# Operands of three routing steps and the scheduler's durations in a fused attention and mixture-of-experts kernel

## The chip, the cores and the metric

The kernel runs on one core of a Trainium2 chip. The metric is device time in microseconds for one execution of the whole program. Engines are named as in the profile: PE (TensorE), DVE (VectorE), ACT (ScalarE), POOL (GpSimd), SP (SyncE, here an issuer of DMAs).

## What is computed

The reference, cut to the parts that bear on the change. Attention and a gated layer produce 2304 tokens of 512 values; then tokens are routed to eight experts, each with room for 288 of them, in the order of their logits.

```python
q_pool = q.reshape(4, 8, 576, 2, 64).mean(axis=3)
attn = softmax(scale * q_pool @ k^T); x = attn @ v      # 2304 tokens x 512
x = ((x @ w1) * (x @ w2) @ w3) @ w_out
logits = x @ w_gate                                      # 2304 x 8
cap = 2304 // 8
for idx in np.argsort(-logits.flatten()):
    tok, e = idx // 8, idx % 8
    if assigned[tok] >= 0 or counts[e] >= cap:
        continue
    assigned[tok] = e; counts[e] += 1
for e in range(8):
    h = np.maximum(x[assigned == e] @ moe2_w1[e], 0.0)
    out[assigned == e] = h @ moe2_w2[e]
```

## The kernel before

Every fp32 product is made of three matmuls on operands split into a high and a low part (names that end in h and l, or hi and lo): hi by hi, lo by hi, hi by lo. The split of a weight block `u` of an expert is `uh` (a rounding copy on ACT) and `ul` (the subtraction `u - uh`, on DVE for experts 0, 1, 6 and 7, on POOL for 2 to 5). SP loads the blocks, 512 KB each, 64 in all, into a few buffers in turn; a buffer is free again when its `ul` has been made.

Attention runs until about 500 us, the gated layer until about 765 us. Then three kinds of work run side by side until about 1064 us:

- the routing, mostly on DVE, with small matmuls on PE;
- the rest of the gated layer, `x2` (matmuls of 512 columns, the last ones of 256), on PE until about 933 us;
- from there the experts on PE: per expert 96 matmuls of 288 columns in layer 1 (`pb<-exh,uh` and the like), 96 in layer 2 (`pb<-ehh,uh`), and transposes of gathered tokens (`g`) and outputs (`ey`).

The routing has eight phases. Each of the phases 0 to 6 searches, for all experts at once, the logit from which on an expert is full. It takes eight rounds: DVE makes a mask (`rt_mask`), PE counts with it (the MASK matmuls `pt<-rt_oh,rt_mask`), DVE multiplies, reduces and compares (`rt_cnt`, `rt_own`), PE spreads the verdict (the OWN8 matmul `pt<-rt_own,rc_ones`), DVE narrows the threshold. The tail of a phase compares with the threshold (`rt_ge`, twice), sums (`rt_rows`), lets PE sum over the partitions (the ROWS matmuls `pt<-rt_rows,...`), runs a scan along each expert's tokens that a row of ones and zeros `rst` resets (`tensor_tensor_scan`), and updates the expert's room left (`rt_r`, `rem`), the logits `L`, the accepted tokens (`rt_acc`, and `A` on POOL) and `pend`, the experts that became full. `pick` then takes one full expert, and `lists` makes the list of its tokens: `sl_all`, `sl_rows`, a PE matmul on it, six `sl_oh`, PE's list matmuls (`pt<-sl_mv,sl_oh`), and from their result `sl_fl` and the index tile `idx`, with which POOL gathers the expert's tokens (`g<-x,idx`) and scatters its outputs. Phase 7 has no search: it adds the experts that never filled to `pend`, picks one and makes its list.

Small operands of the routing lie in SBUF tiles (`ring`) or in a PSUM bank (`at`, printed as `pt` in the profile). The order on each engine is fixed before the program is built: the class `Sched` takes all operations of this stage with an engine, a modelled duration and a priority, runs a list schedule in model time, and every engine then executes its instructions in that order. The modelled duration on DVE is 65 ns and 1.04 ns for each element of a partition; what is called a duration in this text's diff is that number of elements (`dve(144, ...)`). Instructions recorded in this way all have the line L113 in the profile.

Of the kernel before, what the change touches and what calls it, by code (L numbers as in the profile page):

```python
# [11 lines left out]
F32 = mybir.dt.float32  # L12
F32R = mybir.dt.float32r
BF16 = mybir.dt.bfloat16
# [761 lines left out]
def routing_consts(nc, pool, spare):  # L776
# [10 lines left out]
    c = {}  # L787
# [12 lines left out]
    c["rst"] = rst = pool.tile([128, 8, 18], F32, name="rc_rst")  # L800
# [75 lines left out]
def routing(nc, sch, rp, slots, bank, c, L, keyL, A, rows_of, idx, prio, prio_l):  # L876
# [6 lines left out]
    def ring(name, n, shape, dt):  # L883
        return make_ring(sch, rp, "rt_" + name, n, shape, dt)
# [11 lines left out]
    r_M, r_M1 = at("M", 1, [128, 1], I32), ring("M1", 1, [128, 1], I32)  # L896
    (grid1, _), (wd, _) = at("grid1", 1, [128, NTHR], I32)(), at("wd", 1, [128, 8], F32)()
# [23 lines left out]
    dve(8, lambda: nc.vector.tensor_copy(wd, c["wd"]), [], ["rt_consts"])  # L921
    dve(144, lambda: nc.vector.tensor_scalar(L, L, -1e34, 1e34, op0=OP.max, op1=OP.min), [keyL], [keyL])

    def pick(n):

        (sc, ksc), (top, kt), (own, ko) = r_sc(), r_top(), r_own()
        dve(8, lambda: nc.vector.scalar_tensor_tensor(sc, pend, 0.5, wd, op0=OP.is_gt, op1=OP.mult), [keyP, "rt_consts"], [ksc], pr=P_PICK)
        dve(8, lambda: nc.vector.tensor_reduce(top, sc, axis=AX.X, op=OP.max), [ksc], [kt], pr=P_PICK)
        dve(8, lambda: nc.vector.tensor_scalar(own, sc, top, None, op0=OP.is_equal), [ksc, kt], [ko], pr=P_PICK)
        dve(8, lambda: nc.vector.tensor_tensor(pend, pend, own, op=OP.subtract), [keyP, ko], [keyP], pr=P_PICK)  # L930
        dve(4, lambda: nc.vector.scalar_tensor_tensor(
            rows_of[n], top[:, :].to_broadcast([128, 4]), -512.0, c["row"], op0=OP.mult, op1=OP.add), [kt], [("rows_of", n)], pr=P_PICK)
        return own, ko

    lists = slot_lists(nc, sch, rp, slots, bank, c, A, idx, prio, prio_l)
    for ph in range(8):
        if ph == 7:
            dve(8, lambda: nc.vector.scalar_tensor_tensor(pend, rem, 1e8, pend, op0=OP.is_lt, op1=OP.add), [keyR, keyP], [keyP])
            own = pick(7)
# [16 lines left out]
        if ph < 7:  # L956
# [4 lines left out]
            for rd, b in enumerate(BITS):  # L961
# [4 lines left out]
                else:  # L966
                    thr, kth = r_thr()
                    if rd == 1:
                        link(T, lambda thr=thr, T=T, rd=rd, base=base: nc.vector.tensor_scalar(
# [11 lines left out]
                if 0 < rd < len(BITS) - 1:  # L981
                    G, kG = r_G()
                    dve(T, lambda G=G, rd=rd, base=base: nc.vector.tensor_scalar(
                        G, c["grid"][rd + 1][0], base, None, op0=OP.bitwise_xor), [kb], [kG])
                    sch.ops[-1].sdeps.add(cut)
# [48 lines left out]
            for x, op in ((0, OP.is_ge), (1, OP.is_equal)):  # L1034
                dve(144, lambda ge=ge, th=th, mu=mu, oh=oh, x=x, op=op: nc.vector.scalar_tensor_tensor(
# [9 lines left out]
            def f(ps=ps, rows=rows):  # L1045
# [7 lines left out]
                inc.rearrange("p e c -> p (e c)"), c["rst"].rearrange("p e c -> p (e c)"),  # L1053
                ge[:, 1].rearrange("p e c -> p (e c)"), 0.0, op0=OP.mult, op1=OP.add), [(kge, 1)], [kin])
# [24 lines left out]
            dve(144, lambda ac2=ac2, s=s: nc.vector.tensor_reduce(  # L1079
# [31 lines left out]
def slot_lists(nc, sch, rp, slots, bank, c, A, idx, prio, prio_l):  # L1111
# [11 lines left out]
    r_mv, r_fl = ring("mv", 2, [128, 2, 3, NC], BF16), ring("fl", 2, [96, 2, 3], F32)  # L1123

    def lists(n, own):
# [7 lines left out]
        dve(144, lambda: nc.vector.tensor_tensor(  # L1133
# [12 lines left out]
        dve(18, lambda: nc.vector.scalar_tensor_tensor(slot, inc, pre, s, op0=OP.add, op1=OP.mult), [ki, kp, ks], [ksl])  # L1146
# [16 lines left out]
        def f2():  # L1163
# [3 lines left out]
        dve(6, lambda: nc.vector.tensor_copy(fl.rearrange("p x g -> p (x g)"), ps2.tile[:96, 0:6]), [], [kf], uses=[ps2])  # L1167
        dve(3, lambda: nc.vector.scalar_tensor_tensor(idx[n], fl[:, 0], 256.0, fl[:, 1], op0=OP.mult, op1=OP.add),
            [kf], [("idx", n)])
# [673 lines left out]
```

## Time and profile before

| what | us |
|---|---|
| median of 3 runs | 1208.83 |
| the runs | 1206.01 to 1209.98 |
| profiled execution, its own time | 1207.23 |
| its span, first to last instruction | 1205.4 |

The profile shows one execution. The busy shares of section 1 of its page are means over the whole span; the stage that the change touches is a fourth of it and is read by windows and timelines. Rows of a timeline show the start of a group of like instructions, its length, engine and operation, output and inputs, their count, and in brackets how long the engine had been idle before and which instruction released it. Durations of matmuls are longer than their distance, since they are pipelined.

### The profile page before, as it was taken

The numbers are of one execution on the slowest core, as the hardware profiler recorded it, in microseconds if no ns is written. First come the engines' busy times: TensorE is split into PE (matmuls) and PEld (weight loads), VectorE is DVE, ScalarE is ACT, GpSimd is POOL, SyncE is SP. The second block draws the span as 40 slices with busy tenths as digits, with TensorE's granted clock in tenths as the row PEclk, the third lists the DMA queues.
The fourth block names the chain that finished last, engine by engine and source line by source line (L and its number), as shares of the span: only waits on it lengthen the run. The fifth ranks groups of instructions, "written<-read, shape, count | busy, mean of one in ns | idle before, by whom it ended". The sixth has DMA issues, their size and how long they took to land.

```text
span 1205.4 us, 24241 instructions
## 1 busy us (share of the span) xinstructions
PE 1155.2 (96%) x8377; PEld 1091.5 (91%) x8377; DVE 946.3 (79%) x2953; ACT 701.8 (58%) x1453; POOL 513.0 (43%) x561
## 2 busy tenths in 40 slices
PE   7999999999999999999999999999999798899996
PEld 5999999999999999899999999776778798899996
DVE  7999999999999999998777765588778988833541
ACT  6888888888888888754433344223222454445520
POOL 4566666666666665500000000224443357776110
PEclk9999999999999999999999999999999899999998
DMA  8676666666666743125556532553112465546520
GB/s 214 153 179 150 154 154 154 154 154 149 158 140 153 161 114 86 42 88 201 188 180 192 187 95 85 165 174 106 40 40 51 152 201 167 175 134 215 176 69 21
DMA packets 114219, 167.92 MB, mean 139 GB/s; under 512 B 47479, under 2 KB 77310, under 8 KB 114094
## 3 DMA queue, kind: packets, MB, share of 16 engines
q1 hardware_dynamic: 110926, 156.92, 48.1%
q0 software_dynamic: 3168, 9.44, 2.5%
q8 instruction: 66, 1.08, 0.4%
q14 instruction: 59, 0.48, 0.1%
HBM read 104.87 MB, written 22.48 MB: 106 GB/s over the span
## 4 chain that ended last, share of the span: by engine, by line
PE 79%; DVE 16%; DMA 2%; issue 1%; SPq 1%; POOL 0%; ACT 0%; DVEq 0%; POOLq 0%; ACTq 0%
PE pb L113 37%; PE s L590 12%; PE pt L614 7%; PE pt L664 6%; PE pt L113 6%; PE s L664 6%; DVE pt L113 4%; PE s L614 3%; DVE sl_oh L113 1%; DVE ul L113 1%; DVE p L600 1%; DVE rt_mask L113 1%; PE pt L543 1%; DVE cv_v L113 1%; DMA u<-in_moe_w_dram 1%
## 5 line engine op out<-in xcount | busy, mean ns | idle before, releaser
L600 DVE TENSOR_SCALAR_CACHE_REDUCE p<-s 128x384 f32<-128x384 f32 x432 | 229.9, 551 | 32.6 <-PE pt L614 12.4
L590 PE MATMUL s<-kst,qst 128*128 128x384 f32 x768 | 199.7, 359 | 4.9 <-DVE p L600 3.4
L605 ACT ACTIVATE p<-p,mn 128x1152 f32<-128x1152 f32 x144 | 181.2, 1258 | 24.0 <-DVE mn L603 22.0
L113 POOL TENSOR_TENSOR x2l<-hraw,x2h 128x512 fp32r<-128x512 f32 x36 | 46.5, 1294 | 301.0 <-PE pt L113 250.7
L113 PE MATMUL pb<-xhi,wh 128*128 128x288 f32 x512 | 155.8, 304 | 1.2 <-ACT wh L113 1.2
L113 PE MATMUL pb<-xhi,wl 128*128 128x288 f32 x512 | 150.9, 295 | 1.4 <-POOL wl L113 1.2
L113 PE MATMUL pb<-xlo,wh 128*128 128x288 f32 x512 | 150.7, 294 | 0.0
L590 PEld LDWEIGHTS s<-kst,qst 128*128 128x128 f32 x768 | 123.4, 190 | 11.0 <-DVE p L600 8.0
L614 PE MATMUL pt<-ident,p 128*128 128x128 f32 x879 | 132.0, 272 | 0.3 <-ACT p L605 0.3
L648 DVE TENSOR_TENSOR p_lo<-pt,p_hi 128x384 fp32r<-128x384 f32 x230 | 124.6, 551 | 0.7 <-ACT p_hi L331 0.7
L331 ACT ACTIVATE p_hi<-pt 128x384 fp32r<-128x384 f32 x230 | 106.7, 493 | 11.2 <-PE pt L614 10.9
L614 PEld LDWEIGHTS pt<-ident,p 128*128 128x128 f32 x879 | 106.7, 140 | 4.5 <-ACT p L605 0.5
L113 PEld LDWEIGHTS pb<-xhi,wh 128*128 128x128 f32 x512 | 96.3, 188 | 2.6 <-ACT wh L113 1.6
L113 PEld LDWEIGHTS pb<-xhi,wl 128*128 128x128 f32 x512 | 96.1, 188 | 1.8 <-POOL wl L113 1.4
L341 POOL TENSOR_TENSOR p_lo<-praw,p_hi 128x384 fp32r<-128x384 f32 x96 | 97.0, 1018 | 0.4
L113 PEld LDWEIGHTS pb<-xlo,wh 128*128 128x128 f32 x512 | 96.4, 188 | 0.0
L113 DVE SCALAR_TENSOR_TENSOR cv_v<-cv_raw,cv_v 128x512 int32<-128x512 int32 (+1 forms) x120 | 83.8, 706 | 5.6 <-ACT cv_raw L113 4.4
L113 ACT ACTIVATE uh<-u 128x1024 fp32r<-128x1024 f32 (+1 forms) x84 | 68.6, 852 | 24.4 <-DMA u<-in_moe_w_dram 21.0
L335 POOL CAST p_hi<-praw 128x384 fp32r<-128x384 f32 x96 | 47.6, 506 | 81.6 <-ACT praw L331 81.5
L113 POOL TENSOR_TENSOR ul<-u,uh 128x1024 fp32r<-128x1024 f32 (+1 forms) x41 | 77.2, 1912 | 9.7 <-ACT uh L113 9.5
L113 PE MATMUL pb<-exh,uh 128*128 128x288 f32 x248 | 78.9, 318 | 0.0
L113 PE MATMUL pb<-ehh,uh 128*128 128x288 f32 x256 | 78.6, 307 | 0.0
(315 smaller groups left out, 3189.5 us busy)
## 6 DMA issues: line engine op xcount, KB each, us to landing
u<-in_moe_w_dram SPq DMA_DIRECT2D x64, 512.0 KB, 3.5
cv_raw<-in_moe_w_dram SPq DMA_DIRECT2D x32, 512.0 KB, 3.9
vr<-in_v_dram SPq DMA_DIRECT2D x32, 288.0 KB, 5.1
kr<-in_k_dram SPq DMA_DIRECT2D x32, 288.0 KB, 5.9
kst<-kH SPq DMA_DIRECT2D x31, 288.0 KB, 4.1
kst<-kL SPq DMA_DIRECT2D x31, 288.0 KB, 5.2
qr<-in_q_dram SPq DMA_DIRECT2D x15, 576.0 KB, 6.2
w3t<-wg SPq DMA_DIRECT2D x16, 512.0 KB, 3.5
```

Source lines behind the costliest of these rows:

```text
L113: return f(*[x.get() if isinstance(x, Lazy) else x for x in a], **{n: x.get() if isinstance(x, Lazy) else x for n, x in k.items()})
L331: nc.scalar.activation(out, in_, AF.Copy)
L335: nc.gpsimd.tensor_copy(out, in_)
L341: (nc.vector if eng == "DVE" else nc.gpsimd).tensor_tensor(out, a, b, op=OP.subtract)
L543: nc.tensor.transpose(ps.tile[:, a * 128:(a + 1) * 128], r[:, 3 * c + a, :, :].rearrange("p h d -> p (h d)"), ident)
L590: nc.tensor.matmul(ps.tile[:, :384], a[:, :], b[:, cs], start=(n == 0), stop=(n == len(passes) - 1))
L600: sch.op("DVE", c_dve(384), lambda ps=ps, c=c, cs=cs: nc.vector.tensor_scalar(t[:, cs], ps.tile[:, :384], 1.0, BIG, op0=OP.mult, op1=OP.mi ...
L605: sch.op("ACT", c_act(S, psum=False, acc=True), lambda: nc.scalar.activation(t, t, AF.Exp, bias=mn[:, 3:4], scale=-1.0, accum_out=sm[0][:, ...
L614: nc.tensor.transpose(ps.tile[:, a * 128:(a + 1) * 128], t[:, b * 128:(b + 1) * 128], ident)
L648: sch.op("DVE", c_dve(384), lambda view=view, src=src: nc.vector.tensor_tensor(view(lo), src(), view(hi).bitcast(F32), op=OP.subtract), us ...
L664: nc.tensor.matmul(ps.tile[:, :n], vt[:, t, :, :], src[half][:, t, off:off + n], start=(half == 0 and t == 0), stop=(half == 1 and t == NT ...
```

## The change

It has two parts. In the first, three steps of the routing read one operand from PSUM that came from SBUF. The reset row `rst` is made in bf16, copied once into the PSUM bank, and the scan reads it there. In phase 7 the step that adds the unfilled experts to `pend` becomes two: a comparison of `rem` that writes into PSUM, and an addition. In `lists`, only half of the list matmuls' result is copied to SBUF (`sl_fl`), and the index step reads the other half from PSUM.

In the second part, seven numbers that the scheduler takes for durations are raised; the instructions themselves stay. These numbers change the order of all engines from 765 us on.

```diff
-    c["rst"] = rst = pool.tile([128, 8, 18], F32, name="rc_rst")
+    c["rst"] = rst = pool.tile([128, 8, 18], BF16, name="rc_rst")
...
+    rst = at("rst", 1, [128, 4 * NC], F32)()[0].bitcast(BF16)
...
+    dve(72, lambda: nc.vector.tensor_copy(rst.bitcast(I32), c["rst"].rearrange("p e c -> p (e c)").bitcast(I32)), [], ["rt_rst"])
     dve(144, lambda: nc.vector.tensor_scalar(L, L, -1e34, 1e34, op0=OP.max, op1=OP.min), [keyL], [keyL])
...
-        dve(8, lambda: nc.vector.tensor_scalar(own, sc, top, None, op0=OP.is_equal), [ksc, kt], [ko], pr=P_PICK)
+        dve(80, lambda: nc.vector.tensor_scalar(own, sc, top, None, op0=OP.is_equal), [ksc, kt], [ko], pr=P_PICK)
...
-            dve(8, lambda: nc.vector.scalar_tensor_tensor(pend, rem, 1e8, pend, op0=OP.is_lt, op1=OP.add), [keyR, keyP], [keyP])
+            open_, kop = r_pen()
+            dve(8, lambda open_=open_: nc.vector.tensor_scalar(open_, rem, 1e8, None, op0=OP.is_lt), [keyR], [kop])
+            dve(8, lambda open_=open_: nc.vector.tensor_tensor(pend, open_, pend, op=OP.add), [kop, keyP], [keyP])
...
-                        link(T, lambda thr=thr, T=T, rd=rd, base=base: nc.vector.tensor_scalar(
+                        link(T + 72, lambda thr=thr, T=T, rd=rd, base=base: nc.vector.tensor_scalar(
...
-                    dve(T, lambda G=G, rd=rd, base=base: nc.vector.tensor_scalar(
+                    dve(T + 72, lambda G=G, rd=rd, base=base: nc.vector.tensor_scalar(
...
-                dve(144, lambda ge=ge, th=th, mu=mu, oh=oh, x=x, op=op: nc.vector.scalar_tensor_tensor(
+                dve(300, lambda ge=ge, th=th, mu=mu, oh=oh, x=x, op=op: nc.vector.scalar_tensor_tensor(
...
-                inc.rearrange("p e c -> p (e c)"), c["rst"].rearrange("p e c -> p (e c)"),
-                ge[:, 1].rearrange("p e c -> p (e c)"), 0.0, op0=OP.mult, op1=OP.add), [(kge, 1)], [kin])
+                inc.rearrange("p e c -> p (e c)"), rst,
+                ge[:, 1].rearrange("p e c -> p (e c)"), 0.0, op0=OP.mult, op1=OP.add), [(kge, 1), "rt_rst"], [kin])
...
-            dve(144, lambda ac2=ac2, s=s: nc.vector.tensor_reduce(
+            dve(255, lambda ac2=ac2, s=s: nc.vector.tensor_reduce(
...
-        dve(144, lambda: nc.vector.tensor_tensor(
+        dve(240, lambda: nc.vector.tensor_tensor(
             al, A.rearrange("p e c -> p c e"), own[:, None, :].to_broadcast([128, NC, 8]), op=OP.mult), ["A", kown], [ka], pr=P_PICK)
...
-        dve(18, lambda: nc.vector.scalar_tensor_tensor(slot, inc, pre, s, op0=OP.add, op1=OP.mult), [ki, kp, ks], [ksl])
+        dve(90, lambda: nc.vector.scalar_tensor_tensor(slot, inc, pre, s, op0=OP.add, op1=OP.mult), [ki, kp, ks], [ksl])
...
-        dve(6, lambda: nc.vector.tensor_copy(fl.rearrange("p x g -> p (x g)"), ps2.tile[:96, 0:6]), [], [kf], uses=[ps2])
-        dve(3, lambda: nc.vector.scalar_tensor_tensor(idx[n], fl[:, 0], 256.0, fl[:, 1], op0=OP.mult, op1=OP.add),
-            [kf], [("idx", n)])
+        dve(3, lambda: nc.vector.tensor_copy(fl, ps2.tile[:96, 3:6]), [], [kf], uses=[ps2])
+        dve(3, lambda: nc.vector.scalar_tensor_tensor(idx[n], ps2.tile[:96, 0:3], 256.0, fl, op0=OP.mult, op1=OP.add),
+            [kf], [("idx", n)], uses=[ps2])
```

The new orders, at three places. The first is DVE's queue at the end of the search of phase 4, where PE passes from `x2` to expert 0: before, from the last threshold step (a write of one word into `pt_68`) to `rt_r`.

```order
L113 SCALAR_TENSOR_TENSOR pt_68<-rt_n_9312,pt_68 128x1
L113 SCALAR_TENSOR_TENSOR rt_ge_9494<-pt_68,rt_oh_9239 128x18x8 x2
L113 TENSOR_REDUCE rt_rows_9501<-rt_ge_9494 128x16
L113 SCALAR_TENSOR_TENSOR pt_68<-rc_rst,rt_ge_9494 128x144
L113 TENSOR_TENSOR ul_11013<-u_9775,uh_10998 128x1024
L113 TENSOR_TENSOR exl_11018<-pt_67,exh_11011 128x288
L113 TENSOR_TENSOR exl_11018<-pt_65,exh_11011 128x288
L113 SCALAR_TENSOR_TENSOR rt_y_9511<-rt_ge_9494,pt_68 128x144
L113 TENSOR_TENSOR rt_r_9515<-pt_66,rt_rem_9180 128x8
```

And with the change, from the third `ul` to `rt_r`; two more `ul` stand in the same round ahead of these rows.

```order
L113 TENSOR_TENSOR ul_11050<-u_9851,uh_11009 128x1024
L113 SCALAR_TENSOR_TENSOR rt_ge_9498<-pt_68,rt_oh_9241 128x18x8 x2
L113 TENSOR_TENSOR ul_11077<-u_11007,uh_11055 128x1024
L113 TENSOR_REDUCE rt_rows_9505<-rt_ge_9498 128x16
L113 SCALAR_TENSOR_TENSOR pt_68<-pt_68,rt_ge_9498 128x144
L113 SCALAR_TENSOR_TENSOR rt_y_9517<-rt_ge_9498,pt_68 128x144
L113 TENSOR_TENSOR ul_11090<-u_11043,uh_11080 128x1024
L113 TENSOR_TENSOR exl_11005<-pt_66,exh_10995 128x288
L113 TENSOR_TENSOR ul_11097<-u_11066,uh_11092 128x1024
L113 TENSOR_TENSOR exl_11005<-pt_66,exh_10995 128x288
L113 TENSOR_TENSOR ul_11128<-u_11085,uh_11110 128x1024
L113 TENSOR_TENSOR rt_r_9521<-pt_66,rt_rem_9180 128x8
```

Seven `ul` now stand ahead of `rt_r`, counted from the last round's mask, and one stood there before. The row on `pt_68` with 128x144 before `rt_y` is the scan.

The second place is phase 7: DVE from `sl_all` of the list before (phase 6's) on, before,

```order
L113 TENSOR_TENSOR sl_all_9569<-A,pt_68 128x144
L113 SCALAR_TENSOR_TENSOR rt_pend_9190<-rt_rem_9180,rt_pend_9190 128x8
L113 TENSOR_TENSOR A<-A,pt_68 128x144
L113 SCALAR_TENSOR_TENSOR pt_68<-rt_pend_9190,pt_68 128x8
L113 TENSOR_REDUCE pt_68<-sl_all_9569 128x18
L113 TENSOR_REDUCE pt_68<-pt_68 128x1
L113 TENSOR_REDUCE sl_rows_9583<-pt_68 128x1
```

and with the change.

```order
L113 TENSOR_TENSOR sl_all_9573<-A,pt_68 128x144
L113 TENSOR_TENSOR rt_pend_9190<-pt_68,rt_pend_9190 128x8
L113 TENSOR_TENSOR A<-A,pt_68 128x144
L113 SCALAR_TENSOR_TENSOR pt_68<-rt_pend_9190,pt_68 128x8
L113 TENSOR_REDUCE pt_68<-sl_all_9573 128x18
L113 TENSOR_REDUCE pt_68<-pt_68 128x1
L113 SCALAR_TENSOR_TENSOR ehl_11247<-pb_6477,ehh_11195 128x288
L113 TENSOR_SCALAR pt_68<-pt_68 128x8
L113 SCALAR_TENSOR_TENSOR rows_12425<-pt_68,rc_row 128x4
L113 TENSOR_REDUCE sl_rows_9589<-pt_68 128x1
```

The step that writes `rt_pend` reads `pt_68` where it read `rt_rem`; two `ehl` (one of them a few rows ahead of this piece), a step of `pick` and `rows` moved ahead of `sl_rows`. PE's queue around the matmul on `sl_rows` of phase 6, before,

```order
L113 MATMUL pb_6536<-exh_11271,uh_0_9687 128x288
L113 MATMUL pb_6536<-exl_11358,uh_0_9687 128x288
L113 MATMUL pb_6536<-exh_11271,ul_0_9746 128x288
L113 LDWEIGHTS rc_tris
L113 MATMUL pt_66<-sl_rows_9583,rc_tris 128x1
L113 MATMUL pt_67<-ident,ey_11341 96x128
L113 MATMUL pt_67<-ident,ey_11356 96x128
L113 MATMUL pt_67<-ident,ey_11440 96x128
L113 MATMUL pt_67<-ident,ey_11480 96x128
```

and with the change.

```order
L113 MATMUL pb_6514<-exh_11210,uh_11145 128x288
L113 MATMUL pb_6514<-exl_11293,uh_11145 128x288
L113 MATMUL pb_6514<-exh_11210,ul_11282 128x288
L113 LDWEIGHTS rc_tris
L113 MATMUL pt_67<-sl_rows_9589,rc_tris 128x1
L113 MATMUL pb_6514<-exh_11210,uh_11181 128x288
L113 MATMUL pb_6514<-exl_11293,uh_11181 128x288
L113 MATMUL pb_6514<-exh_11210,ul_11322 128x288
L113 MATMUL pb_6514<-exh_11210,uh_0_9645 128x288
L113 MATMUL pb_6514<-exl_11293,uh_0_9645 128x288
```

Twelve transposes of `ey`, of which four stood right behind `sl_rows` in the piece before, now stand ahead of it with 39 matmuls of expert work since the ROWS matmuls (42 before). From there on, 15 and 42 such matmuls follow up to the list matmuls of phase 6 (before: 12 transposes, 6 and 24), and 24 matmuls and 9 transposes from these to those of phase 7 (before: 24).

The third place is POOL in phase 5, where it starts on expert 2's weights, before,

```order
L113 TENSOR_TENSOR ul_0_9798<-u_11459,uh_0_9785 128x512
L113 TENSOR_TENSOR ul_1_9817<-u_11459,uh_1_9794 128x512
L113 TENSOR_TENSOR ul_11013<-u_11485,uh_10998 128x1024
L113 TENSOR_TENSOR ul_11036<-u_11534,uh_11016 128x1024
L113 TENSOR_TENSOR ul_11094<-u_11607,uh_11022 128x1024
L113 TENSOR_TENSOR ul_11107<-u_11640,uh_11073 128x1024
L113 TENSOR_TENSOR ul_11114<-u_11674,uh_11098 128x1024
L113 TENSOR_TENSOR A<-A,rt_acc_9529 128x144
L113 TENSOR_TENSOR ul_11194<-u_11711,uh_11141 128x1024
```

and with the change.

```order
L113 TENSOR_TENSOR ul_1_9837<-u_11394,uh_1_9793 128x512
L113 TENSOR_TENSOR ul_10997<-u_11512,uh_10983 128x1024
L113 TENSOR_TENSOR ul_11026<-u_11535,uh_11003 128x1024
L113 TENSOR_TENSOR ul_11050<-u_11561,uh_11009 128x1024
L113 TENSOR_TENSOR ul_11077<-u_11615,uh_11055 128x1024
L113 TENSOR_TENSOR ul_11090<-u_11649,uh_11080 128x1024
L113 TENSOR_TENSOR ul_11097<-u_11680,uh_11092 128x1024
L113 TENSOR_TENSOR ul_11128<-u_11721,uh_11110 128x1024
L113 TENSOR_TENSOR A<-A,rt_acc_9533 128x144
L113 TENSOR_TENSOR ul_11282<-u_11755,uh_11145 128x1024
```

`A` stood behind two `ul` of 512 columns and five of 1024; now one of 512 and seven of 1024 stand ahead of it, and another one of 512 columns ahead of three scatters before these rows.

## Rows read from the trace of the kernel before

**Rows 1.** Page, section 1: busy us, share of span, instructions.
```profile
PE 1155.2 (96%) x8377; PEld 1091.5 (91%) x8377; DVE 946.3 (79%) x2953; ACT 701.8 (58%) x1453; POOL 513.0 (43%) x561
```

**Rows 2.** Waits of TensorE, 765 to 1064: us in total, times, longest.
```profile
PE pt L113 <- DVE exl L113: 5.4, 2, 2.9
PE pt L113 <- DVE rt_oh L113: 4.6, 5, 1.2
```

**Rows 3.** TensorE timeline: start, us, what, xcount [idle before, releaser].
```profile
998.15 0.20 PE L113 MATMUL pt<-rt_rows,rc_neg 128*128 128x8 bf16 x2 [2.94 <-DVE exl L113]
...
1047.86 0.16 PE L113 MATMUL pt<-sl_rows,rc_tris 128*128 128x1 bf16 x1 [3.58 <-DVE sl_rows L113]
...
1061.62 1.86 PE L113 MATMUL pt<-sl_mv,sl_oh 128*96 128x6 bf16 x15 [2.26 <-DVE sl_oh L113]
```

**Rows 4.** Windows: us, busy of PE, PEld, DVE, ACT, POOL; PEclk, DMA, GB/s.
```profile
933.00:948.00 15.00, 8.60 (x54) 7.72 (x53) 13.56 (x43) 6.35 (x9) 6.05 (x6) 0.77 0.43 134
997.00:1002.00 5.00, 3.85 (x22) 3.83 (x22) 4.73 (x17) 1.76 (x4) 0.91 (x2) 0.66 0.47 173
1049.00:1053.00 4.00, 4.00 (x20) 3.84 (x20) 3.73 (x15) 1.40 (x4) 2.84 (x7) 0.57 0.75 274
```

**Rows 5.** VectorE timeline, 985 to 1070.
```profile
993.69 4.06 DVE L113 TENSOR_TENSOR_SCAN pt<-rc_rst,rt_ge 128x144 f32<-128x144 f32 x1
...
1004.92 0.42 DVE L113 TENSOR_TENSOR sl_all<-A,pt 128x144 f32<-128x144 f32 x1
...
1037.98 0.46 DVE L113 TENSOR_TENSOR_SCAN pt<-rc_rst,rt_ge 128x144 f32<-128x144 f32 x1
...
1042.06 0.18 DVE L113 TENSOR_SCALAR pt<-rt_U 128x18 f32<-128x18 f32 x1
...
1044.44 2.18 DVE L113 SCALAR_TENSOR_TENSOR rt_pend<-rt_rem,rt_pend 128x8 f32<-128x8 f32 x1
...
1048.29 0.14 DVE L113 TENSOR_TENSOR rt_pend<-rt_pend,pt 128x8 f32<-128x8 f32 x1
...
1053.26 0.46 DVE L113 SCALAR_TENSOR_TENSOR ehl<-pb,ehh 128x288 fp32r<-128x288 f32 x1 [0.43 <-ACT ehh L113]
...
1056.44 4.75 DVE L113 SCALAR_TENSOR_TENSOR idx<-sl_fl 96x3 int32<-96x3 f32 x1
1061.12 1.90 DVE L113 TENSOR_TENSOR sl_oh<-pt,rc_i 128x288 bf16<-128x288 f32 x5
```

**Rows 6.** GpSimd timeline, 985 to 1070.
```profile
984.41 13.01 POOL L113 TENSOR_TENSOR ul<-u,uh 128x512 fp32r<-128x512 f32 x6
1000.45 0.49 POOL L113 TENSOR_TENSOR A<-A,rt_acc 128x144 f32<-128x144 f32 x1 [3.03 <-DVE rt_acc L113]
...
1041.88 4.71 POOL L113 TENSOR_TENSOR ul<-u,uh 128x1024 fp32r<-128x1024 f32 x2
...
1056.48 4.70 POOL L113 TENSOR_TENSOR ul<-u,uh 128x1024 fp32r<-128x1024 f32 x2
```

**Rows 7.** Chain that ended last, behind the routing: start, us, what.
```profile
1071.87 11.95 PE pb L113 x90
...
1096.73 0.74 PE pt L113 x9
```

**Rows 8.** Timelines of VectorE, ScalarE, GpSimd, TensorE: phases 2, 4, 5.
```profile
869.37 0.16 DVE L113 TENSOR_TENSOR rt_r<-pt,rt_rem 128x8 f32<-128x8 f32 x1
...
874.23 0.27 PE L113 MATMUL pt<-rt_oh,rt_mask 128*90 128x48 bf16 x3 [0.88 <-DVE rt_oh L113]
...
938.08 1.21 DVE L113 TENSOR_TENSOR ul<-u,uh 128x1024 fp32r<-128x1024 f32 x1
...
943.36 1.06 ACT L113 ACTIVATE uh<-u 128x1024 fp32r<-128x1024 f32 x1 [4.67 <-DMA u<-in_moe_w_dram]
...
979.19 0.68 DVE L113 TENSOR_TENSOR ul<-u,uh 128x512 fp32r<-128x512 f32 x1
...
983.16 7.25 POOL L113 TENSOR_TENSOR ul<-u,uh 128x512 fp32r<-128x512 f32 x4
```

More of the change, by code (lines that the diff above doesn't have):

```diff
@@ L1122, in slot_lists @@
     r_oh, r_og = ring("oh", 1, [128, NC, 96], BF16), ring("og", 1, [128, NC, 3], F32)
-    r_mv, r_fl = ring("mv", 2, [128, 2, 3, NC], BF16), ring("fl", 2, [96, 2, 3], F32)
+    r_mv, r_fl = ring("mv", 2, [128, 2, 3, NC], BF16), ring("fl", 2, [96, 3], F32)
     def lists(n, own):
```

## Prediction

> **What bounds the kernel now.** I read the profile page first: TensorE is busy for 96% of the span, VectorE for 79% [rows 1]. So a change pays only where TensorE stands still, or where it runs at the lower of its two clock levels. Next I asked which waits stop it in the stage that the change touches, from 765 us, where routing starts, to 1064 us, where the last list is made. The table of waits names VectorE in its longest rows [rows 2]. Then I looked at the three longest of these gaps: 2.94 us at 998, 3.58 us at 1048, 2.26 us at 1062 [rows 3]. After the first two the granted clock falls to its lower level: the mean is 0.66 over 997 to 1002 and 0.57 over 1049 to 1053 [rows 4], which costs 5 x 0.34 and 4 x 0.43, 1.7 us each. I take the same behind the third, where the clock falls too.
>
> What was VectorE doing? Each time one instruction took many times its usual length [rows 5]. The scan, 0.46 us in phase 6, took 4.06 us in phase 5; the step on `pend` took 2.18 us where another of its size takes 0.14; the index step, on 96 x 3 elements, took 4.75 us. (A row gives start and length: 993.69 + 4.06 = 997.75.) All three read both operands from SBUF. Beside each, GpSimd ran subtractions `ul`, and the long instruction ended when that row of subtractions ended [rows 6]: 997.75 against 997.42, 1046.62 against 1046.59, 1061.19 against 1061.18. In the same stretches instructions with one operand in PSUM keep their length, such as the 0.14 us one in [rows 5]. So the trace bears out that these three wait for GpSimd, and that reading one operand from PSUM frees them.
>
> **The change part by part.** All terms are against the profiled execution, 1207.2 us, which is 1.6 below the median and inside the runs' spread of 4 us. About 0.3% of the time, 3.6 us, is what a measurement can tell from no change.
>
> *The scan of phase 5.* It shrinks by 4.06 - 0.46 = 3.6 us. TensorE's gap behind it, 2.94 us, goes, and with it the 1.7 us of half clock: **-4.6**. Bounds: 0 (the wait stays) and -4.6. Next late there would be GpSimd's `A`, see the first rival.
>
> *The index step of phase 7.* It shrinks by 4.6 us; behind it stand the five `sl_oh` for which TensorE waited 2.26 us. What hides the new chain is 24 matmuls and 9 transposes between the two groups of list matmuls, about 3.9 us at the pace of [rows 7] (90 matmuls in 11.95 us, 0.133 each; 9 transposes in 0.74, 0.082 each), against six `sl_oh` of 0.38 us [rows 5] and the two steps on `sl_fl` and `idx`, some 2.7 us, on VectorE. The gap and the clock loss go: 2.26 + 1.7, **-4.0**; bounds 0 and -4.0.
>
> *The step on `pend`.* It is split in two: 2.18 becomes about twice 0.16, 1.9 less. But in the new order two `ehl` of 0.46 us each [rows 5] and two small steps, 0.2 each by their like, now stand ahead of `sl_rows`, for which TensorE waits. And TensorE does twelve transposes before that wait instead of behind it, worth 1.0 us, with three matmuls fewer, 0.4. (Only one of the `ehl` and both small steps come behind the `pend` step; the other `ehl` comes shortly before it, on the same chain.) The wait becomes 3.58 - 1.9 + 0.9 + 0.4 - 0.6 = 2.4 us. A gap of 2.26 us still halved the clock, so I give back only the idle time: **-1.2**, with bounds 0 and -5.3 (all of the gap and of the clock).
>
> *The tails of phases 0 to 3.* The raised durations put four more 512-column matmuls between a phase's last round and the next phase's first, where TensorE waits for `rt_oh`, 4.6 us in five waits [rows 2]. Two of the four stand ahead of the ROWS matmuls and so delay the chain that they cover; two stand behind. I take half of it for four phases: **-1.8**, bounds 0 and -3.6.
>
> *The turn from `x2` to the experts (phase 4).* Here the order moves most. Four phases with four more matmuls each empty `x2` one round earlier, and expert 0 starts a round earlier in routing's terms. VectorE gets seven `ul` ahead of `rt_r` where it had one [rows 8]. I worked this out from the mask of the last round, M. In the trace the first `ul` ends at 938.08 + 1.21 = 939.29 and gives its buffer to the fourth's weights; ScalarE's `uh` on these starts at 943.36, after waiting 4.67 us for the load. So one turn of the buffers takes 4.1 (load) + 1.06 (`uh`) + 1.22 (`ul`) = 6.4 us. In the new order the first `ul` ends at M + 1.8, the fourth can end at M + 8.2, and the seventh, whose buffer the fourth frees, at M + 14.8. `rt_r` comes then, where before it came right after the first. The next mask follows 4.9 us later, as in phase 2 (`rt_r` at 869.37, TensorE's mask matmul at 874.23), near M + 20. TensorE meanwhile has 48 matmuls of expert 0 ahead of ROWS and 51 behind (before: none and 48), so it reaches that mask near M + 16.5 and waits some 3.6 us, where it waited 2.4 (`exl`, the 5.4 less 2.9 in [rows 2]). From 933 to 948 TensorE was busy for 8.60 of 15 us at a clock of 0.77 [rows 4]; of the 6.4 us idle I take 0.6 off, since the ROWS matmuls now have work ahead of them and the other stops stay. So 1.2 - 0.6: **+0.6**. The bounds are wide: -4 if the clock stays up (15 x 0.23 = 3.4) and the stops shrink once more by 0.6, +6 if the clock is lost for as long again and the mask's wait doubles (3.4 + 2.4).
>
> *Additions.* One copy of 72 words in the head of routing, with the `rc_wd` copy now ahead of the first step on `L`, and dependences on them: by 0.14 to 0.18 us for a small step [rows 5] that is **+0.5** with a wait, bounds +0.2 and +1.0. The scan's reset row from PSUM I price at nothing, since the steps with a PSUM operand in [rows 5] are as short as those without; the index step's copy gets smaller. [...]
>
> Sum: -4.6 - 4.0 - 1.2 - 1.8 + 0.6 + 0.5 = -10.5, so 1207.2 - 10.5 = **1196.7 us**. A cross-check by TensorE's own work: behind the last group of list matmuls the new order leaves 54 matmuls of 0.133 us and 9 transposes less, 7.9 us; the groups would have to come 2.6 us sooner to give the same.
>
> **The rivals.**
>
> *GpSimd's `A` takes the scan's place.* In phase 5 `A` stood behind two half and five full `ul`, which ended at 997.42 [rows 6]; now one half and seven full, 2.4 us each, stand there in one row, so it may come some 4 us later, and `sl_all` behind it waits. VectorE had 4 us to spare at `A` (1000.45 to 1004.92), of which the shorter scan takes 3.6. For it: the row is longer. Against: expert 2's `ul` may start earlier. Price: up to 2 us of wait and the 1.7 of clock: **1200**.
>
> *More gain.* The transition loses its half clock and the `pend` gap falls under what halves it: -4.6 (0.6 to -4) and -4.1 (-1.2 to -5.3) on the sum: **1188**.
>
> *The operands don't free it.* If the new instructions wait as the old did, only the order counts: -1.8 + 0.6 + 0.5, and -0.6 for the transposes ahead of `sl_rows`: **1206**. The row nearest to the new `pend` step is `TENSOR_SCALAR` from `rt_U` into PSUM, 0.18 us at 1042.06, beside a GpSimd row of `ul` [rows 5, 6]; it did not wait. [...]
>
> *Slower: VectorE's own `ul` get caught.* They read `u` and `uh`, both from SBUF, and are untouched. Expert 1's last one ended at 979.19 + 0.68 [rows 8], 3.3 us before GpSimd's row for expert 2 began at 983.16. The experts now run 51 matmuls, 6.8 us, ahead of routing. If GpSimd's row starts before that last `ul`, VectorE is held until the row ends, as the scan was. Price: a row of seven `ul` of 2.4 us is 16.8, less the 0.7 of its own length, plus 1.7 of clock: 1196.7 + 17.8 = **1214**. It decides from an overlap on; with a row as in [rows 6], 13.01, it would end at 1210. Against it: in the new order GpSimd still does a single `ul` and three scatters before the row.
>
> **How the numbers follow.** My case 0.58, `A` 0.14, more gain 0.12, not freed 0.09, caught 0.07. My case's own range is 1191 to 1203, from the transition's +6 and the bounds of the `pend` and tail terms; the range 1187 to 1206.5 takes in the first three and most of the fourth. Faster than 1205.2: the first three less 0.05 for their upper ends, plus 0.02: 0.81. Within 0.3%: 0.05 + 0.06 = 0.11. Slower than 1212.5: the last case's 0.07 and 0.01 for a bad turn, 0.08.
>
> **What would show it.** All seven scans near 0.46 us and all eight index steps near 0.16; no `exl` or `sl_oh` gap over 1 us at phases 5 and 7; a gap for `sl_rows` of 2 to 3 us, still with half clock; `rt_r` of phase 4 some 14 us behind its mask, with a wait for `uh` before it. Wrong if a scan or index step is still several us long, if `sl_all` waits for `A`, or if a `ul` on VectorE takes more than 2 us.

## The result, and the profile after

| kernel | median us | runs | ratio to before, 95% interval |
|---|---|---|---|
| before | 1209.35 | 4 | |
| changed | 1197.2 | 4 (1190.61 to 1198.9) | 0.9898 [0.9861, 0.9934] |
| changed, again, beside 29 runs of before | 1199.37 | 12 (1196.52 to 1204.84) | 0.9930 [0.9907, 0.9953] |

The change makes the kernel 8 to 12 us faster by these ratios; a time of 1196.7 was forecast. The execution profiled first is the fastest of them, 1190.61 us with a span of 1188.7, so its rows show more gain than the medians. These are, of the changed kernel, section 1 of the page and then the waits of TensorE from 765 to 1064 us (in total, times, longest):

```profile
PE 1148.6 (97%) x8377; PEld 1085.6 (91%) x8377; DVE 934.5 (79%) x2955; ACT 702.7 (59%) x1453; POOL 518.3 (44%) x561
```

```profile
PE pt L113 <- DVE rt_own L113: 3.1, 7, 0.9
PE pt L113 <- DVE rt_oh L113: 3.0, 5, 0.7
...
PE pt L113 <- DVE exl L113: 1.7, 1, 1.7
PE pt L113 <- DVE sl_rows L113: 1.6, 1, 1.6
PE pt L113 <- DMA g<-x,idx: 1.2, 1, 1.2
```

Against [rows 2] the wait for `exl` fell from 5.4 to 1.7 us, that for `rt_oh` from 4.6 to 3.0. The wait for `sl_oh` is no longer there; the one for `sl_rows` was 3.58 [rows 3] and is 1.6. TensorE's timeline at what remains in phases 5 and 7:

```profile
984.20 0.21 PE L113 MATMUL pt<-rt_own,rc_ones 98*128 98x120 f16 x1 [0.92 <-DVE rt_own L113]
...
1043.47 0.18 PE L113 MATMUL pt<-sl_rows,rc_tris 128*128 128x1 bf16 x1 [1.62 <-DVE sl_rows L113]
```

Windows of the turn, behind the 984 gap, at `sl_rows` and at the last list (columns as in [rows 4]):

```profile
930.00:945.00 15.00, 9.82 (x59) 8.80 (x60) 13.53 (x37) 7.60 (x11) 6.92 (x6) 0.77 0.59 197
982.00:987.00 5.00, 4.08 (x33) 3.94 (x32) 3.46 (x15) 3.15 (x7) 4.27 (x2) 1.00 0.56 170
1043.00:1047.00 4.00, 3.53 (x27) 3.47 (x28) 3.86 (x20) 0.64 (x2) 3.98 (x4) 1.00 0.80 225
1057.00:1062.00 5.00, 5.00 (x42) 5.00 (x41) 0.77 (x3) 1.86 (x4) 4.86 (x5) 1.00 0.63 213
```

The clock, at 0.66 and 0.57 in [rows 4], is full at all three places behind the turn. VectorE's and GpSimd's timelines, for comparison with [rows 5, 6]:

```profile
994.78 0.45 DVE L113 TENSOR_TENSOR_SCAN pt<-pt,rt_ge 128x144 f32<-128x144 bf16 x1
...
1001.39 0.42 DVE L113 TENSOR_TENSOR sl_all<-A,pt 128x144 f32<-128x144 f32 x1
...
1038.38 0.17 DVE L113 TENSOR_SCALAR pt<-rt_rem 128x8 f32<-128x8 f32 x1
...
1041.44 0.16 DVE L113 TENSOR_TENSOR rt_pend<-pt,rt_pend 128x8 f32<-128x8 f32 x1
...
1052.73 0.15 DVE L113 SCALAR_TENSOR_TENSOR idx<-pt,sl_fl 96x3 int32<-96x3 f32 x1
...
1057.29 0.16 DVE L113 SCALAR_TENSOR_TENSOR idx<-pt,sl_fl 96x3 int32<-96x3 f32 x1
```

```profile
993.00 4.77 POOL L113 TENSOR_TENSOR ul<-u,uh 128x1024 fp32r<-128x1024 f32 x2 [0.21 <-ACT uh L113]
997.74 0.48 POOL L113 TENSOR_TENSOR A<-A,rt_acc 128x144 f32<-128x144 f32 x1
...
1037.24 2.40 POOL L113 TENSOR_TENSOR ul<-u,uh 128x1024 fp32r<-128x1024 f32 x1
...
1051.40 9.76 POOL L113 TENSOR_TENSOR ul<-u,uh 128x1024 fp32r<-128x1024 f32 x6 [0.79 <-ACT uh L113]
```

The scan of phase 5 (994.78) and the last two index steps (1052.73 for the list of phase 6, whose index step was the one held for 4.75 us in [rows 5], and 1057.29 for that of phase 7) run inside GpSimd's rows of `ul` (993.00 to 997.77, 1051.40 to 1061.16) and take 0.45, 0.15 and 0.16 us. The comparison of `rem` (1038.38), with its result in PSUM, takes 0.17 beside the `ul` from 1037.24. That is the plainest sign that the operand in PSUM frees them. The addition to `pend` (1041.44) met no `ul` in this order, so its 0.16 us says nothing. On VectorE the turn went as worked out:

```profile
933.25 0.44 DVE L113 TENSOR_TENSOR rt_mask<-pt,rt_thr 128x270 bf16<-128x270 f32 x1
933.80 1.22 DVE L113 TENSOR_TENSOR ul<-u,uh 128x1024 fp32r<-128x1024 f32 x1
...
947.67 1.22 DVE L113 TENSOR_TENSOR ul<-u,uh 128x1024 fp32r<-128x1024 f32 x1 [1.64 <-ACT uh L113]
948.81 0.16 DVE L113 TENSOR_TENSOR rt_r<-pt,rt_rem 128x8 f32<-128x8 f32 x1
```

`rt_r` comes 15.6 us behind the last round's mask (forecast 14.8), behind seven `ul`, the last of which waited 1.64 us for its `uh`.

All gaps of TensorE over 0.15 us from 760 us on sum to 27.1 us before and 15.0 after; the time at half clock (in 1 us windows from 700 to 1180 us the granted clock is 1.00 or 0.50, and between them where it changes), summed over these windows as the missing share, is 10.2 against 3.4 us. Together that is 19 us, where the spans differ by 16.7.

### The profile page after: what moved, and what is told of

It is laid out like the page before. It is cut to its first block, busy times and chain, and to the rows that moved or that the text cites. A ratio compares the mean times of both kernels' runs of the same rounds, so it can differ in the third digit from the quotient of the medians.

```text
span 1188.7 us, 24244 instructions
## 1 busy us (share of the span) xinstructions
PE 1148.6 (97%) x8377; PEld 1085.6 (91%) x8377; DVE 934.5 (79%) x2955; ACT 702.7 (59%) x1453; POOL 518.3 (44%) x561
## 4 chain that ended last, share of the span: by engine, by line
PE 80%; DVE 12%; DMA 3%; issue 2%; ACT 1%; POOL 1%; SPq 0%; DVEq 0%; POOLq 0%; ACTq 0%
PE pb L113 37%; PE s L590 13%; PE pt L614 7%; PE pt L664 6%; PE pt L113 6%; PE s L664 5%; PE s L614 3%; DVE pt L113 3%; DMA u<-in_moe_w_dram 1%; DVE sl_oh L113 1%; DVE p L600 1%; DVE rt_mask L113 1%; DVE ul L113 1%; PE pt L543 1%; DVE cv_v L113 1%
```

## The experiments

**Theory.** The three steps are held by GpSimd's subtractions as long as two operands are in SBUF; freeing them is worth 9.8 of the 10.5 us, and the order little. **Rival.** The order pays: it fills the tails, and takes the steps out of GpSimd's rows.

**1. The changed kernel again** (no edit).

> The changed kernel once more, to see how far its executions spread. Its profiled execution took 1190.6 us, the other runs 1196 to 1199. Theory: the same static order stands still for 14 to 15 us between 765 us and the end each time; where an execution is 6 to 8 us slower, TensorE's clock fell behind one or two more of the gaps (1.7 us each) and a gap near a DMA landing grew by some us. Rival: the executions differ before 765 us, in attention, and the change has no part in it; then the gaps from 765 us on would be the same and the start of routing (765 us) would be later. Median expected: 1196 to 1198.

The ratio is 0.9930 and the median 1199.37 us, 1.4 above what was expected. The profiled execution has a span of 1196.0, 7.3 more than the first. Until 500 us both keep TensorE busy alike (487.97 and 487.19 us), and routing starts at 765 us in both (`rt_pend` is set to zero at 765.24 and 765.71). From 760 us on the gaps are 19.2 against 15.0 us, and the half clock 6.8 against 3.4. So the theory held on where executions differ, not on how little: the largest difference is in phase 5. From the timelines of TensorE, VectorE, ScalarE and GpSimd of this execution:

```profile
986.26 0.21 PE L113 MATMUL pt<-rt_own,rc_ones 98*128 98x120 f16 x1 [2.75 <-DVE rt_own L113]
```

```profile
985.05 0.46 DVE L113 SCALAR_TENSOR_TENSOR ehl<-pb,ehh 128x288 fp32r<-128x288 f32 x1 [3.44 <-ACT ehh L113]
```

```profile
983.66 1.06 ACT L113 ACTIVATE uh<-u 128x1024 fp32r<-128x1024 f32 x1 [4.08 <-DMA u<-in_moe_w_dram]
```

```profile
975.05 2.21 POOL L113 DMA_INDIRECT out_dram<-eo,idx  x1 [0.23 <-issue]
...
978.51 3.65 POOL L113 TENSOR_TENSOR ul<-u,uh 128x512 fp32r<-128x512 f32 x2
```

And SyncE's loads (`q` marks an instruction that only issues a transfer):

```profile
979.83 2.69 SPq L113 DMA_DIRECT2D u<-in_moe_w_dram  x3
```

Read backwards: TensorE waits 2.75 us for `rt_own` (0.92 in the first execution); VectorE's `rt_own` stands behind an `ehl` that waits 3.44 us for ScalarE; ScalarE's `ehh` stands behind a `uh` that waits 4.08 us for its load. The next loads were issued from 979.83 on, 3.8 us before that `uh` began, when the first of the two `ul` from 978.51 had ended. These `ul` came late since three scatters stood ahead of them on GpSimd, one 2.21 us long. In the first execution the same scatters took 0.98, 0.92 and 1.62 us (here 1.50, 2.21 and 0.92), and the load was issued at 978.33. That this load is the one that the `uh` waited for is read from the order of the issues.

**2. The order with the old operands, pend step split.** The scan's and the index step's operands go back to SBUF (the reset row stays in bf16, here and in 8 and 10), and the comparison writes to SBUF:

```diff
+    rst_sb = c["rst"].rearrange("p e c -> p (e c)")
...
-            open_, kop = r_pen()
+            open_, kop = rp.tile([128, 8], F32, name="rt_open"), r_pen()[1]
...
-                inc.rearrange("p e c -> p (e c)"), rst,
+                inc.rearrange("p e c -> p (e c)"), rst_sb,
...
-        dve(3, lambda: nc.vector.scalar_tensor_tensor(idx[n], ps2.tile[:96, 0:3], 256.0, fl, op0=OP.mult, op1=OP.add),
+        dve(3, lambda: nc.vector.scalar_tensor_tensor(idx[n], fl[:, 0], 256.0, fl[:, 1], op0=OP.mult, op1=OP.add),
```

> The new order (all seven raised durations and the two extra instructions) with the three old operands: scan, index step and pend step read both operands from SBUF. Theory (the operands matter, the waits are for GpSimd's subtractions): the scan of phase 5 falls into a row of ul again and takes 2 to 4 us, an index step at the end of phase 6 or 7 takes 4 to 8 us, the pend step is free here because no ul runs beside it in the new order; time 1202 to 1209. Rival (the order is what paid, by 5 us or more from fuller tails and the turn at phase 4): scan and index step stay short because the new order takes them out of GpSimd's rows; time 1196 to 1199.

The ratio is 1.0013 [0.9988, 1.0037], the time 1209.89 us. From VectorE's timeline:

```profile
1024.34 4.31 DVE L113 SCALAR_TENSOR_TENSOR idx<-sl_fl 96x3 int32<-96x3 f32 x1
...
1053.95 2.25 DVE L113 TENSOR_SCALAR rt_open<-rt_rem 128x8 f32<-128x8 f32 x1
```

The theory seemed to hold, with one index step over 4 us, although the scan of phase 5 took 0.96 us where 2 to 4 were expected. But the second row is a step that neither kernel has: the comparison of `rem`, one operand, written to SBUF, was held too, where the theory had it free. So this run may not show the order alone (see 10).

**3. The operands with the old order.** All seven numbers go back, as in

```diff
-                dve(300, lambda ge=ge, th=th, mu=mu, oh=oh, x=x, op=op: nc.vector.scalar_tensor_tensor(
+                dve(144, lambda ge=ge, th=th, mu=mu, oh=oh, x=x, op=op: nc.vector.scalar_tensor_tensor(
```

> The three new operands with the old durations, so the order of before with two more small instructions. Theory (operands): no scan over 0.5 us, no index step over 0.2 us, the gaps for exl at phase 5 (2.94) and for sl_oh at phase 7 (2.26) gone, the gap for sl_rows at most 1.8 us, tails as before with 0.85 us for rt_oh each; 11 to 12 us less than before: 1197 to 1199. Rival (order): less than half of the gain, 1203 to 1207.

The ratio is 0.9918 [0.9895, 0.9942], the time 1197.59 us, as the theory has it. There is no scan over 0.456 us, no index step over 0.158, and at the end of routing one gap over 1 us is left:

```profile
1042.77 0.16 PE L113 MATMUL pt<-sl_rows,rc_tris 128*128 128x1 bf16 x1 [1.80 <-DVE sl_rows L113]
```

**4. The kernel before without `ul` on GpSimd.**

```diff
-        lo_e = ("POOL",) if FILLED <= n < BESIDE else ("DVE",)
+        lo_e = ("DVE",)
```

> The kernel before with every subtraction ul of the experts on VectorE, none on GpSimd; the operands of the three steps are the old ones, both in SBUF. Theory: all seven scans take 0.45 to 0.47 us, all eight index steps 0.14 to 0.17 and the pend step about 0.16, since GpSimd runs nothing beside them but short steps. Rival (it is the operands' place by itself, or DMA traffic into SBUF at that time, that makes them long): some of them stay over 1 us. VectorE gets some 20 us more work on experts 2 to 5, so the time itself says little: 1200 to 1225 us.

The one execution took 1196.68 us, beside a median of 1208.84 for 29 of the kernel before (the fastest 1200.02); 1200 to 1225 had been expected. The groups of scans and index steps (count, shortest/median/longest ns, first and last start), and the `pend` step from VectorE's timeline:

```profile
L113 DVE TENSOR_TENSOR_SCAN pt<-rc_rst,rt_ge x7: 452/456/777, 797.7 to 1049.6; 128x144 f32<-128x144 f32 x7
```

```profile
L113 DVE SCALAR_TENSOR_TENSOR idx<-sl_fl x8: 148/159/236, 817.2 to 1079.8; 96x3 int32<-96x3 f32 x8
```

```profile
1058.07 0.15 DVE L113 SCALAR_TENSOR_TENSOR rt_pend<-rt_rem,rt_pend 128x8 f32<-128x8 f32 x1
```

With both operands in SBUF the longest is 0.78 us; 4.06, 4.75 and 2.18 are gone. It is GpSimd's subtractions on the experts' weights that hold them. The edit changes the order too, so this rests as well on the steps above that stay short inside GpSimd's rows. (The scan of 0.78 us is that of phase 3, as long in the kernel before, at 903.26; GpSimd then made an `x2l` of the gated layer, from 902.42 to 903.71. That this held it wasn't tried.)

**5 and 6. Scan alone, index step alone, with the comparison written to SBUF.** Experiment 3 with the other two steps as in 2.

> The order of before, and of the three new operands only the scan's: the scan reads its reset row from PSUM, index and pend step read SBUF as before. Theory (each term stands alone): all scans 0.46 us, the gap of 2.94 us at phase 5 and its clock loss gone, the waits for sl_rows and sl_oh at phase 7 there as before or a little shifted; 4.6 us less than before: 1203 to 1206. Rival (the terms hang together: the routing that the scan no longer holds up runs into the same row of ul with its index step): the sum of the remaining long instructions grows by 2 us or more and the gain is under 2 us.

> The order of before, and of the three new operands only the index step's. Theory: all index steps 0.15 us, the gap of 2.26 us for sl_oh in phase 7 and its clock loss gone, the scan of phase 5 still about 4 us long; 4.0 us less than before: 1204 to 1206. Rival: the lists are not what the end waits for; gain under 2 us.

The ratios are 0.9989 [0.9976, 1.0001] and 0.9985 [0.9967, 1.0003], as the rivals have it. But in the first, VectorE, GpSimd and TensorE show

```profile
1040.53 4.90 DVE L113 TENSOR_SCALAR rt_open<-rt_rem 128x8 f32<-128x8 f32 x1
```

```profile
1040.67 4.71 POOL L113 TENSOR_TENSOR ul<-u,uh 128x1024 fp32r<-128x1024 f32 x2
```

```profile
1049.37 0.16 PE L113 MATMUL pt<-sl_rows,rc_tris 128*128 128x1 bf16 x1 [6.28 <-DVE sl_rows L113]
```

The comparison alone was held 4.90 us (4.90 in the other run too), and the gap for `sl_rows` grew from 3.58 to 6.28 us in both. What was to be taken away came in by another step, one of the experiment's own making.

**7 and 8. Scan alone and index step alone, the other steps as before.** The `pend` step is the one instruction of before:

```diff
-            open_, kop = r_pen()
-            dve(8, lambda open_=open_: nc.vector.tensor_scalar(open_, rem, 1e8, None, op0=OP.is_lt), [keyR], [kop])
-            dve(8, lambda open_=open_: nc.vector.tensor_tensor(pend, open_, pend, op=OP.add), [kop, keyP], [keyP])
+            dve(8, lambda: nc.vector.scalar_tensor_tensor(pend, rem, 1e8, pend, op0=OP.is_lt, op1=OP.add), [keyR, keyP], [keyP])
```

> The kernel before with the scan's operand alone changed; index step and pend step word for word as before (in the earlier run of this kind the pend step was split in two with the comparison written to SBUF, and that comparison was held for 4.9 us, so it did not show the scan alone). Theory: scan 0.45 us in all phases, no gap and no clock loss at phase 5, pend step about 2 us and an index step over 4 us as before; 4.6 us less than before: 1203 to 1206. Rival (what the scan gives back is taken again by the next wait): gap for sl_rows 2 us or more longer than 3.6, gain under 2 us.

> The kernel before with the index step's operand alone changed, the other two word for word as before. Theory: index steps 0.15 us, no gap for sl_oh, the scan of phase 5 and the pend step long as before; 4.0 us less than before: 1204 to 1206. Rival: gain under 2 us, as in the earlier run of this kind, whose held comparison would then not be what took the gain.

Scan alone: 0.9961 [0.9942, 0.9980], 4.7 us less at before's 1209.6. Index step alone: 0.9945 [0.9924, 0.9965], 6.7 us less. Each is a gain of its own. In the scan's run the other two are as long as in [rows 5]:

```profile
1044.33 2.18 DVE L113 SCALAR_TENSOR_TENSOR rt_pend<-rt_rem,rt_pend 128x8 f32<-128x8 f32 x1
...
1056.26 4.78 DVE L113 SCALAR_TENSOR_TENSOR idx<-sl_fl 96x3 int32<-96x3 f32 x1
```

The index step's run gave more than its term; in its profile the scan of phase 5, both operands in SBUF, was 1.82 us long, not 4.06 (1.49 in 6), though from phase 2 up to there VectorE and GpSimd run the order of before. So a part can come from that shorter scan, which the edit leaves alone.

**9. Scan and index step.** Both edits together.

> The kernel before with the scan's and the index step's operands changed, the pend step as before. Theory: the two terms add, 8.6 us less than before, 1199 to 1202, and the pend step, still 1 to 2.5 us long, is what separates it from the run with all three operands (11.3 us less). Rival: the pend step falls out of GpSimd's row once the scan is short, then it costs nothing and this run equals the one with all three, 1197 to 1199.

The ratio is 0.9917 [0.9895, 0.9938], 10.2 us between the medians. The time, 1199.37 us, lies in the theory's range, but the ratio is that of experiment 3, as the rival has it. The rival's mechanism did not come: the `pend` step is still 2.18 us long and TensorE's gap is

```profile
1046.91 0.16 PE L113 MATMUL pt<-sl_rows,rc_tris 128*128 128x1 bf16 x1 [3.57 <-DVE sl_rows L113]
```

against 1.80 in experiment 3. The 1.8 us don't show in the ratios, which their intervals of some 2.6 us to a side allow. In this profile the clock did not fall behind the gap, where it did behind the same gap in 7 (3.58 us, at 1047.75). Windows behind it, of 9 and then of 7 (columns as in [rows 4]):

```profile
1047.00:1052.00 5.00, 5.00 (x40) 4.71 (x40) 4.83 (x22) 2.08 (x5) 2.83 (x7) 1.00 0.61 199
```

```profile
1048.00:1052.00 4.00, 4.00 (x22) 3.73 (x21) 3.85 (x18) 1.78 (x3) 1.97 (x7) 0.57 0.57 200
```

So the 1.7 us that the sum takes for the clock are not the price of every such gap.

**10. The order alone, all three steps as before.** Experiment 2 with the one `pend` instruction of 7.

> The new order with all three steps as before (pend step in one instruction; in the earlier run of this kind it was split and its comparison held for 2.25 us). Theory (the order alone gains nothing): tails 0.63 us for rt_oh, an index step of 4 us at the end of phase 6 or 7 with a gap for rt_own or sl_rows of 3 us or more, a gap of 2.7 to 3.1 us for rt_own in phase 5; 1205 to 1210. Rival (the order is worth the 3.7 us of its tails once the held comparison is gone): 1201 to 1204.

The ratio is 0.9924 [0.9900, 0.9948], the time 1200.04 us, better than the theory and the rival. The held steps, with the index step of phase 5 ahead of them, GpSimd at the later one, and TensorE's gap:

```profile
1017.90 0.31 DVE L113 SCALAR_TENSOR_TENSOR idx<-sl_fl 96x3 int32<-96x3 f32 x1
...
1038.21 2.35 DVE L113 TENSOR_TENSOR_SCAN pt<-rc_rst,rt_ge 128x144 f32<-128x144 bf16 x1
...
1059.63 1.07 DVE L113 SCALAR_TENSOR_TENSOR idx<-sl_fl 96x3 int32<-96x3 f32 x1
```

```profile
1058.31 6.01 POOL L113 TENSOR_TENSOR ul<-u,uh 128x1024 fp32r<-128x1024 f32 x3 [0.79 <-ACT uh L113]
```

```profile
1048.83 0.18 PE L113 MATMUL pt<-sl_rows,rc_tris 128*128 128x1 bf16 x1 [3.05 <-DVE sl_rows L113]
```

Steps with two SBUF operands still meet GpSimd, but now the longest take 0.96 (twice), 2.35, 1.07 and 1.05 us, not 4.06, 2.18 and 4.75; the scan of phase 5 takes 0.96, and the gaps for `exl` of phase 5 and for `sl_oh` are gone. The `pend` step, at 1046.81 beside a scatter, took 0.15. The steps were held for less here.

The order alone does not see to that, for experiment 2 had the same one: TensorE, ScalarE and GpSimd run the same instructions in the same order in both from the start of routing on, and VectorE too up to the comparison. Yet there the index step of phase 5 took 4.31 us (0.31 here), and TensorE waited behind it and for `sl_rows`:

```profile
1029.77 0.26 PE L113 MATMUL pt<-rt_own,rc_ones 98*128 98x120 f16 x1 [3.77 <-DVE rt_own L113]
...
1060.94 0.19 PE L113 MATMUL pt<-sl_rows,rc_tris 128*128 128x1 bf16 x1 [3.04 <-DVE sl_rows L113]
```

The gap behind the held comparison, 3.04, is as long as the 3.05 without it. So in these two profiles the held comparison adds nothing to TensorE's wait, and the longest wait came ahead of it. Why all runs of 10 are faster than those of 2 isn't shown.

So the two parts of the change can be two remedies for the same waits: the operands alone give 0.9918, the order alone 0.9924 in this build and 1.0013 with the split comparison, both 0.9898 and 0.9930.

**11. All `ul` on VectorE, in the changed kernel**, with the edit of 4.

> The changed kernel, and all subtractions ul on VectorE. If GpSimd's rows of ul are what still costs in the new order (the loads of expert 2 wait for buffers that GpSimd frees late, behind three scatters: 2.75 us for rt_own and a clock loss in the second execution), that gap goes, the tails keep 0.63 us for rt_oh, and the time falls to 1190 to 1194. Rival: VectorE, with some 20 us more to do between 980 and 1100, becomes late for the experts: more waits for ehl and exl, 1197 to 1205.

**12. VectorE's `ul` up to expert 3**, in the changed kernel.

```diff
-FILLED = 2
+FILLED = 4
```

> The changed kernel with VectorE doing the subtractions of experts 2 and 3 too and GpSimd only those of 4 and 5. By the same theory the late loads of expert 2 go while VectorE gets only half of the extra work: 1190 to 1195, at or below the run with none on GpSimd. Rival: the last DVE ul of expert 3 now meets GpSimd's first ul of expert 4, both reading two operands from SBUF, and one of them is held for 2 us or more: 1196 to 1202.

The results are 0.9858 [0.9835, 0.9881], 1192.56 us, and 0.9878 [0.9856, 0.9899], 1195.82 us. The first beats both kernels; its interval lies below that of the changed kernel's second set of runs and overlaps that of the first. In its profile the gaps from 962 to 1085 us sum to 1.6 us (3.1 and 6.3 in the two executions of the changed kernel), and the one for `sl_rows` is

```profile
1069.13 0.16 PE L113 MATMUL pt<-sl_rows,rc_tris 128*128 128x1 bf16 x1 [0.88 <-DVE sl_rows L113]
```

so the wait for expert 2's blocks is gone, as the theory of 1 has it, and VectorE has room for the work: its `ul` of 1024 columns takes 1.2 us, GpSimd's 2.4. The theory of the second had it at or below the first, which the medians don't bear out; its rival did come once, a `ul` on VectorE of 2.56 us at 1097.09 beside one on GpSimd (1096.14 to 1098.56).

## Why the prediction was right, and where its sum was not

**The bound and the reading of the long instructions** were right: with GpSimd's subtractions away all three are short (0.78, 0.24 and 0.15 us at most, 4), with one operand in PSUM scan and index step are short inside GpSimd's rows (0.45, 0.15 and 0.16 us, the profile after). One row that the prediction leans on does not bear it out, though: GpSimd stood idle around the 0.14 us step at 1048.29, as its next row shows. The step from 1042.62, inside GpSimd's row from 1041.88 [rows 6], is the one to name. From the timelines of GpSimd and VectorE in the kernel before:

```profile
1049.66 0.28 POOL L113 TENSOR_TENSOR sl_og<-sl_ge 128x54 f32<-128x54 f32 x1 [3.08 <-DVE sl_ge L113]
```

```profile
1042.62 0.17 DVE L113 SCALAR_TENSOR_TENSOR pt<-rt_pend,pt 128x8 f32<-128x8 f32 x1
```

**Scan**, -4.6: alone -4.7 (7). **Index step**, -4.0: alone -6.7 with an interval that begins at -4.2 (8). Both, -8.6: about -10, interval -7.5 to -12.7 (9). The mechanism was right. The index step's run gave more than its term, but there the scan was short too, so how much of it is the step's own stays open.

**The step on `pend`**, -1.2: its gap was forecast at 2.4 us, with half clock. It is 1.6 in the first execution, with full clock, and 2.0 in the second, with the clock lost from 1049 to 1052. Experiment 3 against 9 shows the shorter gap (1.80 against 3.57 us), but nothing of it in the time. In the new order the step needed no help: with both operands in SBUF it took 0.15 us (10).

**Tails**, -1.8: the waits for `rt_oh` fell by 1.6 us, and all gaps from 760 to 925 us from 7.4 to 3.7, the far bound of the term.

**Turn**, +0.6: of 15 us 5.2 were idle instead of 6.4, at the same clock of 0.77. `rt_r` came nearly as late as worked out (the working itself adds up to 14.6 us, not 14.8). But the wait of 3.6 us at the next mask did not come there: TensorE lost 1.7 us for `exl`, 1.2 for a gather and 0.9 for `ehl` on the way to it, 3.8 in all. And before, the clock fell a second time, behind the wait for `exl` that ended at 948.90:

```profile
950.00:954.00 4.00, 4.00 (x22) 3.96 (x21) 2.91 (x14) 2.03 (x4) 2.68 (x3) 0.57 0.90 285
```

In both executions of the changed kernel it is full there (1.00), a gain of 1.7 us that the term lacks. All gaps from 925 to 962 us sum to 7.3 before and to 7.5 and 7.8 after, so with the clock the term had the wrong sign in these profiles.

**Additions**, +0.5: from the zeroing of `rt_pend` to the first scan 31.74 us passed before (764.64 to 796.38) and 31.65 after (765.71 to 797.36), so nothing of the term shows.

**What failed is the price of the order**, in the rival "the operands don't free it": -1.8 + 0.6 + 0.5 - 0.6, 1206 us. The order alone gave 1200.0, some 9 us less than before (10), or nothing, 1209.9 (2). I had kept the three held steps at their old lengths and moved only what stands around them. How long such a step is held changes, even within one order: 4.31 and 0.31 us for one index step in one order (2, 10), 4.06, 1.82 and 1.49 for the scan of phase 5 in the order of before. Nor may the terms be added: with the steps free the order had nothing left to save there. On top of the operands it gave nothing that the intervals show (3 against 1); in the second execution its late loads for expert 2 took back in phase 5 what its tails gave. The forecast of 1196.7 stands because the operands' part, 9.8 of the 10.5 us, carries it by itself; that the misses of the small terms, to both sides, left the total where it was is luck.

**Rivals.** GpSimd's `A` did come behind the longer row, at 997.74, but `sl_all` followed only at 1001.39: no wait. VectorE's own `ul` were not caught for long: the longest of the first execution took 1.50 us instead of 1.22, beside a GpSimd row that ended at 1088.17, and the kernel before had one of 1.60.

```profile
1087.76 1.50 DVE L113 TENSOR_TENSOR ul<-u,uh 128x1024 fp32r<-128x1024 f32 x1 [2.76 <-ACT uh L113]
```

"More gain" fits the first execution alone.

## What to carry to other kernels

Where VectorE and GpSimd run side by side, look for single short instructions that take microseconds (4.06, 2.18 and 4.75 us here), and try one operand, or the only result, in PSUM before you touch the order: in this kernel that was worth as much as the whole new order at its best (ratios of 0.9918 and 0.9924), and the steps so changed were short. In the first execution of the changed kernel the scans took at most 0.456 us and the index steps at most 0.157, inside GpSimd's rows too; in experiment 3 it was 0.456 and 0.158. Don't add the prices of two remedies for one wait; make the sum for each alone. When an experiment puts a step back, put back the very instruction: a split form with its result in another memory made a wait of its own here, 4.90 us long, which hid the effect in two runs.

## What the hardware showed that I had not expected

A `tensor_scalar` on 128x8 fp32 elements, with a single operand, was held 4.90, 4.90 and 2.25 us when it wrote to SBUF (5, 6, 2), and took 0.17 us with the result in PSUM, beside the `ul` from 1037.24 (the profile after, 1038.38).

How long a step is held is not settled. In the kernel before the index step sat out two subtractions (4.75 us, 2.35 to 2.4 each); in experiment 10 it was let in behind one, at 1059.63 + 1.07 = 1060.70, while GpSimd's row from 1058.31 went on. In experiment 5 the comparison began at 1040.53, 0.14 us before GpSimd's first `ul`, and still sat out both. No run here shows what decides this.
